# Softmax-band convolution and soft mixture of experts: softmax taps skewed by matmuls and GpSimd in place of a DRAM round trip

## The chip, the cores and the metric

The kernel runs on one core of one Trainium2 chip. The metric is device time in microseconds, the median of several executions. Everything is float32. A core has TensorE (PE; its weight loads are shown as PEld), VectorE (DVE), ScalarE (ACT), GpSimd (POOL) and SyncE (SP), which here only issues DMAs.

## The reference

Two layers follow each other. The first weights seven consecutive rows of `x` by a softmax over seven taps, separately for each token and head; the second is a soft mixture of experts.

```
# x: (8, 3584, 192); weight_gen: (8, 3584, 8 heads, 7 taps); a head has 24 channels
w   = softmax(weight_gen, axis=-1)                 # exp(w - max) / (sum + 1e-9)
out[b, s, head] = sum_k w[b, s, head, k] * x_padded[b, s + k, head]   # 6 zero rows ahead
x      = out.reshape(28672, 192)
logits = x @ phi                                   # 32 slots
d      = softmax over all tokens;  slot_in = d.T @ x
slot_out = relu(slot_in @ w1[e]) @ w2[e]           # 8 experts, 4 slots each
y      = softmax over slots(logits) @ slot_out
```

## The kernel before

**Tiling.** A batch has 35 groups of 4 x 26 = 104 tokens. A block is 26 tokens, which read 32 rows of `x`. Seven groups are a supergroup (40 in all), two groups are a pair (140 in all), eight pairs are a unit (17 units and a last one of four pairs). The convolution of a block and of four heads is one matmul: the weights are a band matrix of 128 x 26 (4 heads x 32 rows of `x`, by 26 tokens), the moving operand is the block's part of `x`, laid out block-diagonally by head in `xbd` (128 x 96). `conv(p)` issues 16 of them for pair p, which use the four column groups of the array side by side and write one of three PSUM buffers `cv`.

**A pair's path.** `conv(p)`, then `conv_out(p)` (ACT copies `cv` to `tm`), then `xpose(p)` (three TensorE transposes to `pt`) and `xpose_out(p)` (ACT copies to `cm`). Transposes run one pair behind the convolution. Per unit follow `logits` (16 matmuls to `ls`), `top` and `save` (DVE), `newmax` (a matmul to `pmx`), `newmax_out` (DVE), `dexp` (ACT), `dturn` (DVE), `dispatch` (16 matmuls to `ac`) and `rescale` (DVE). `soft` makes the softmax over slots per half batch, in steps on DVE (max), POOL (subtract), ACT (exp), DVE (sum, reciprocal) and POOL (multiply).

**The taps.** Taps arrive laid out by token. A band needs them skewed: row i of `x` holds tap i - j for token j. For the first two supergroups the kernel builds bands directly (`taps_*`, `band_mult`, DVE block transposes `band_turn`). For the others it works in chunks of two supergroups: `chunk_top` (DVE max), `chunk_sub` (POOL), `chunk_exp` (ACT), `chunk_sum` (POOL), `chunk_inv` (DVE), `chunk_norm` (POOL); then `send` writes the chunk to a DRAM buffer `via` with eight DMAs, each with the row offset that makes the skew, and `fetch` reads it back as `rows`, and `band_make` (DVE) multiplies `rows` by a mask that lies in the PSUM tile `pmx`:

```
SY.dma_start(via[ch % 2][q : q + 128].rearrange("(m k) s l -> m k s l", k=KS)
             [:, 0:KT, q], exps[ch % NEXP][q::KS, 0:KT])
```

**Order.** The engines' queues are written out by hand. A list `todo` of steps with planned times, made from `CONV`, `XPOSE`, `LOGITS`, `DISPATCH`, is sorted, and the steps are issued in that order; each engine runs its own in order, and semaphores hold it where an input is not there. The planned times set the order alone. SP issues all DMAs in the order of the list, so a DMA that waits holds up those behind it. `loadx(s + 2)` overwrites a buffer of `x` that supergroup s has finished with.

**The end.** After the last unit come the experts' small matmuls, and an output phase in which `rows` matmuls, copies on ACT and DVE and DMAs to the result alternate.

Of the kernel before, what the change touches and what calls it, by code (L numbers as in the profile page):

```python
# [8 lines left out]
F32 = mybir.dt.float32  # L9
# [7 lines left out]
KS = 8  # L17
FAR = -1e30
CG = 14
# [8 lines left out]
L = 2 * NBC  # L28
NCH = B * NG // CG
# [15 lines left out]
def conv_soft_moe(ctx, tc, xh, w0, wh, phi, w1a, w1b, w2, out):  # L45
# [15 lines left out]
    XB = 4 * NBC * GW  # L61
# [13 lines left out]
    def soft(pool, h, step):  # L75
        g0, n = HALVES[h]
        lt = LT[:, g0 : g0 + n, :]
        if step == 0:
            rms[h] = pool.tile([128, 18, 1], F32, tag="rm", name=f"rm{h}")[:, 0:n]
            V.tensor_reduce(out=rms[h], in_=lt, axis=AX.X, op=ALU.max)  # L80
        elif step == 1:
            G.tensor_tensor(out=lt, in0=lt, in1=rms.pop(h).to_broadcast([128, n, NS]),  # L82
                            op=ALU.subtract)
        elif step == 2:
            A.activation(lt, lt, AF.Exp)
        elif step == 3:
            sm = sms[h] = pool.tile([128, 18, 1], F32, tag="sm", name=f"sm{h}")[:, 0:n]
            sp = sm if pool is not pa else smP[h % 2][:, 0:n]
            V.tensor_reduce(out=sp, in_=lt, axis=AX.X, op=ALU.add)
            V.tensor_scalar_add(sm, sp, EPS)  # L90
            V.reciprocal(sm, sm)  # L91
# [13 lines left out]
    NXB, NTM, NCV, NRAW, NEXP, NBAND = 2, 2, 3, 2, 2, 3  # L105
    xbd = [big[:, i * XB : (i + 1) * XB].rearrange("p (h c) -> p h c", h=4) for i in range(NXB)]

    HB = NBC // 2
    WB = HB * 32
    early = w1a_sb.rearrange("p e f -> p (e f)")  # L110
    at = [0]

    def part(b, k):
        at[0] += b * k
        return early[:, at[0] - b * k : at[0]].rearrange("p (b k) -> p b k", k=k)

    wgs = [part(NBC, KS) for _ in range(2)]
    ens = [part(NBC, KS + 1) for _ in range(2)]
    wts = [part(HB, 32) for _ in range(2)]
    Ws = {(s, hf): part(HB, 32) for s in range(2) for hf in range(2)}  # L120

    raws = [fix.tile([128, L, KT], F32, name=f"raw{i}") for i in range(NRAW)]
    exps = [fix.tile([128, KS, L], F32, name=f"exp{i}") for i in range(NEXP)]
    rows8 = [fix.tile([128, KS, L], F32, name=f"rows{i}") for i in range(2)]
    bands = [fix.tile([128, HB, T, 2], F32, name=f"band{i}") for i in range(NBAND)]
    dram = actx.enter_context(tc.tile_pool(name="dram", bufs=1, space=bass.MemoryType.DRAM))
    via = [dram.tile([128 + KS, KS, L], F32, name=f"via{i}") for i in range(2)]

# [4 lines left out]

    pmx = ps_l.tile([128, 512], F32, name="pmx")
    pm, maskP = pmx[:, 0:5], pmx[:, 64:128].rearrange("p (i o) -> p i o", o=2)
    qnegP, q0P = pmx[:, 128:132], pmx[:, 132:133]
    smP = [pmx[:, 160 + 32 * i : 192 + 32 * i].rearrange("p (g o) -> p g o", o=1) for i in range(2)]
# [6 lines left out]
    G.memset(rows8[0], 0.0)  # L146
# [7 lines left out]
    for t in ens:  # L154
        V.memset(t[:, :, KS:], EPS)
    for t in exps:
        V.memset(t[:, KT], EPS)
    V.memset(xbd[0][:, 0, :], 0.0)
    V.memset(dd[:, 4:], 0.0)
    for h in (1, 2):  # L160
        G.memset(xbd[0][:, h, :], 0.0)
    A.copy(xbd[0][:, 3, :], zero.to_broadcast([128, NBC * GW]))
    A.copy(xbd[1][:, 0, :], zero.to_broadcast([128, NBC * GW]))
# [7 lines left out]
    maskT = keep.tile([128, 1, 32], F32, name="maskT")  # L171
    ident = keep.tile([128, 128], F32, name="ident")
    make_identity(nc, ident)

# [6 lines left out]
    mq = keep.tile([128, 5], F32, name="mq")  # L181

    for t in tms:
        V.memset(t[:, :, 0:1], 1.0)
        V.memset(t[:, :, 2 * D + 1 : 2 * D + 2], 1.0)
    V.memset(qneg, 0.0)
    V.memset(q0, 0.0)
    V.memset(q0[0:32], 1.0)
    for q in range(4):
        V.memset(qneg[32 * q : 32 * q + 32, q : q + 1], -1.0)  # L190

    def loadx(s):
        xb = xbd[s % NXB]
        for h in range(4):
            SY.dma_start(xb[32 * h : 32 * h + 32, h, :], xh[s, h])  # L195

    def loadw0(s):
        SY.dma_start(wgs[s], w0[s])

    def loadw(ch):  # L200
        SY.dma_start(raws[ch % NRAW], wh[ch - 1])

    tops, sums = {}, {}

    def chunk_top(ch):

        tops[ch] = pa.tile([128, L, 1], F32, tag="top", name=f"top{ch}")
        V.tensor_reduce(out=tops[ch][:, :, 0], in_=raws[ch % NRAW], axis=AX.X, op=ALU.max)  # L208

    def chunk_sub(ch, eng=G):  # L210
        raw = raws[ch % NRAW]
        eng.tensor_tensor(out=raw, in0=raw, in1=tops.pop(ch).to_broadcast([128, L, KT]),  # L212
                          op=ALU.subtract)

    def chunk_exp(ch):
        A.activation(exps[ch % NEXP][:, 0:KT], raws[ch % NRAW].rearrange("p b k -> p k b"), AF.Exp)  # L216

    def chunk_sum(ch, eng=G):
        e = exps[ch % NEXP]
        t = sums[ch] = pa.tile([128, 4, L], F32, tag="tree", name=f"sum{ch}", bufs=1)  # L220
        eng.tensor_tensor(out=t, in0=e[:, 0:4], in1=e[:, 4:KS], op=ALU.add)  # L221
        eng.tensor_tensor(out=t[:, 0:2], in0=t[:, 0:2], in1=t[:, 2:4], op=ALU.add)
        eng.tensor_tensor(out=t[:, 0], in0=t[:, 0], in1=t[:, 1], op=ALU.add)  # L223

    def chunk_inv(ch):
        t = sums[ch]
        V.reciprocal(t[:, 0], t[:, 0])  # L227

    def chunk_norm(ch, eng=G):
        w = exps[ch % NEXP][:, 0:KT]  # L230
        eng.tensor_tensor(out=w, in0=w, in1=sums.pop(ch)[:, 0:1].to_broadcast([128, KT, L]),  # L231
                          op=ALU.mult)

    def send(ch, lo=0, hi=KS):

        for q in range(lo, hi):
            SY.dma_start(via[ch % 2][q : q + 128].rearrange("(m k) s l -> m k s l", k=KS)  # L237
                         [:, 0:KT, q], exps[ch % NEXP][q::KS, 0:KT])

    def fetch(ch):  # L240
        SY.dma_start(rows8[ch % 2], via[ch % 2][0:128])

    def band_make(s):

        r = rows8[s // 2 % 2][:, :, s % 2 * NBC : (s % 2 + 1) * NBC]
        r = r.rearrange("p q (b o) -> p b q o", o=2)
        for j in range(0, T, KS):
            k = min(KS, T - j)
            V.tensor_tensor(out=bands[s % NBAND][:, :, j : j + k], in0=r[:, :, 0:k],  # L249
                            in1=maskP[:, j : j + k].rearrange("p (o q) t -> p o q t", o=1)  # L250
                            .to_broadcast([128, HB, k, 2]), op=ALU.mult)

    def taps_top(s, lo=0, n=NBC):
        mx = pa.tile([128, NBC, 1], F32, tag="wmx", name=f"wmx{s}_{lo}")[:, 0:n]
        V.tensor_reduce(out=mx[:, :, 0], in_=wgs[s][:, lo : lo + n], axis=AX.X, op=ALU.max)
        return mx

    def taps_exp(mx, s, lo=0, n=NBC, eng=V):
        en = ens[s][:, lo : lo + n, 0:KS]
        i = eng.tensor_tensor(out=en, in0=wgs[s][:, lo : lo + n],  # L260
                              in1=mx.to_broadcast([128, n, KS]), op=ALU.subtract)
        A.activation(en, en, AF.Exp)
        return i

    def taps_sum(s, lo=0, n=NBC):
        sm = pa.tile([128, NBC, 1], F32, tag="wsm", name=f"wsm{s}_{lo}")[:, 0:n]
        V.tensor_reduce(out=sm[:, :, 0], in_=ens[s][:, lo : lo + n], axis=AX.X, op=ALU.add)
        V.reciprocal(sm, sm)
        return sm

    def taps_norm(sm, s, lo=0, n=NBC, eng=G):
        en = ens[s][:, lo : lo + n, 0:KS]
        eng.tensor_tensor(out=en, in0=en, in1=sm.to_broadcast([128, n, KS]), op=ALU.mult)

    def band_mult(wt, s, at, lo, n, eng):
        wn = ens[s][:, at + lo : at + lo + n, 0:KS]
        eng.tensor_tensor(out=wt[:, lo : lo + n].rearrange("p b (a q) -> p b a q", q=KS),
                          in0=wn.rearrange("p b (o q) -> p b o q", o=1)
                          .to_broadcast([128, n, 32 // KS, KS]),
                          in1=mask.rearrange("p o (a q) -> p o a q", q=KS)  # L280
                          .to_broadcast([128, n, 32 // KS, KS]),
                          op=ALU.mult)

    def band_tiles(s, hf):
        return wts[(2 * s + hf) % 2], Ws[s, hf]

    turns = []
# [153 lines left out]
    for t in via:  # L441
        SY.dma_start(t[0:128], rows8[0])
# [444 lines left out]
```

## Time and profile before

| | |
|---|---|
| median of 3 executions | 410.22 us (410.08 to 415.51) |
| the profiled execution | 414.09 us, span 412.0 us |
| PE, DVE, ACT, POOL busy | 79%, 57%, 48%, 37% of the span |
| mean granted TensorE clock | 0.865 of full speed |
| bytes moved by DMA | 88.88 MB, mean 216 GB/s; 23792 of 43186 packets under 512 B |

The profile was taken of one execution, which lasted 414.09 us; its own span from the first to the last instruction is 412.0 us, and what is said of stages refers to it. Busy shares are averages over stages with different limits: a start until about 40 us, the convolution until about 328 us, then the experts and the output, where DMA moves about 400 GB/s.

### The profile page before, as it was taken

The numbers are of one execution on the slowest core, as the hardware profiler recorded it, in microseconds if no ns is written. First come the engines' busy times: TensorE is split into PE (matmuls) and PEld (weight loads), VectorE is DVE, ScalarE is ACT, GpSimd is POOL, SyncE is SP. The second block draws the span as 40 slices with busy tenths as digits, with TensorE's granted clock in tenths as the row PEclk, the third lists the DMA queues.
The fourth block names the chain that finished last, engine by engine and source line by source line (L and its number), as shares of the span: only waits on it lengthen the run. The fifth ranks groups of instructions, "written<-read, shape, count | busy, mean of one in ns | idle before, by whom it ended". The sixth has DMA issues, their size and how long they took to land.

```text
span 412.0 us, 15274 instructions
## 1 busy us (share of the span) xinstructions
PE 324.9 (79%) x6624; PEld 223.1 (54%) x6624; DVE 236.5 (57%) x500; ACT 199.1 (48%) x390; POOL 153.1 (37%) x147
## 2 busy tenths in 40 slices
PE   7664984949785986683989689789989998989940
PEld 7443663737563754463767467567767765323310
DVE  8954625464754682635567675567665354976540
ACT  7462453626444653443576565675566410634420
POOL 7732452527454563261545465543121142000000
PEclk9685898888988898977799999999999999995555
DMA  7547569698786798756488747766664690899996
GB/s 233 159 111 188 149 167 222 163 217 224 210 219 193 195 254 221 196 166 171 126 232 223 195 133 224 222 165 172 170 174 134 252 370 2 317 399 399 401 400 259
DMA packets 43186, 88.88 MB, mean 216 GB/s; under 512 B 23792, under 2 KB 24176, under 8 KB 43120
## 3 DMA queue, kind: packets, MB, share of 16 engines
q1 hardware_dynamic: 43120, 87.91, 71.0%
q8 instruction: 52, 0.85, 0.9%
q14 instruction: 14, 0.11, 0.1%
HBM read 56.98 MB, written 30.91 MB: 213 GB/s over the span
## 4 chain that ended last, share of the span: by engine, by line
PE 33%; DMA 27%; DVE 12%; SPq 11%; ACT 7%; issue 4%; POOL 3%; ACTq 0%; DVEq 0%; POOLq 0%
PE cv L312 10%; DMA via<-exp 8%; DMA out<-big 7%; PE pt L331 6%; DMA big<-xh 6%; PE ls L360 5%; SPq L195 5%; SPq L237 4%; PE ac L425 4%; DMA raw<-wh 4%; ACT exp L216 4%; DVE band L249 3%; PE po L771 2%; DMA w1b_sb<-w1b 2%; DMA rows<-via 2%
## 5 line engine op out<-in xcount | busy, mean ns | idle before, releaser
L312 PE MATMUL cv<-big,band 128*26 128x96 f32 x4256 | 125.9, 262 | 24.4 <-DMA big<-xh 10.8
L312 PEld LDWEIGHTS cv<-big,band 128*26 128x26 f32 x4256 | 97.7, 112 | 47.6 <-issue 24.9
L319 ACT COPY tm<-cv 128x384 f32<-128x384 f32 x140 | 67.2, 480 | 93.7 <-PE cv L312 93.1
L331 PE MATMUL pt<-ident,tm 122*128 122x122 f32 x420 | 80.3, 304 | 25.6 <-ACT tm L319 25.5
L249 DVE TENSOR_TENSOR band<-rows,pmx 128x448 f32<-128x448 f32 (+1 forms) x152 | 70.1, 523 | 31.7 <-DMA rows<-via 27.7
L331 PEld LDWEIGHTS pt<-ident,tm 122*128 122x128 f32 x420 | 47.7, 154 | 47.1 <-ACT tm L319 28.2
L336 ACT COPY cm<-pt 128x312 f32<-128x312 f32 x139 | 58.3, 420 | 3.3 <-PE pt L331 3.1
L216 ACT ACTIVATE exp<-raw 128x784 f32<-128x784 f32 x19 | 31.4, 1654 | 36.6 <-DMA via<-exp 31.8
L771 PE MATMUL po<-cT,so 32*128 32x442 f32 (+3 forms) x256 | 45.5, 785 | 2.0 <-ACT big L778 1.0
L231 POOL TENSOR_TENSOR exp<-exp,sum 128x784 f32<-128x784 f32 x18 | 33.5, 1860 | 29.4 <-DVE sum L227 14.1
L212 POOL TENSOR_TENSOR raw<-raw,top 128x784 f32<-128x784 f32 x18 | 28.2, 1565 | 34.3 <-DVE top L208 22.5
L778 ACT COPY big<-po 128x936 f32<-128x936 f32 (+1 forms) x24 | 21.8, 917 | 33.3 <-DMA out<-big 16.5
L221 POOL TENSOR_TENSOR sum<-exp 128x448 f32<-128x448 f32 x17 | 19.3, 1137 | 49.1 <-ACT exp L216 49.1
L778 DVE COPY big<-po 128x936 f32<-128x936 f32 (+1 forms) x24 | 26.1, 1095 | 16.6 <-DMA out<-big 12.5
L82 POOL TENSOR_TENSOR LT<-LT,rm 128x576 f32<-128x576 f32 (+1 forms) x16 | 18.1, 1131 | 41.9 <-DVE rm L80 41.9
L360 PE MATMUL ls<-cm,phi_sb 128*32 128x208 f32 (+1 forms) x576 | 30.3, 353 | 2.7 <-ACT cm L336 2.0
L771 PEld LDWEIGHTS po<-cT,so 32*128 32x128 f32 (+1 forms) x256 | 15.7, 202 | 30.6 <-ACT big L778 11.1
L425 PE MATMUL ac<-tm,dt 128*32 128x193 f32 x544 | 28.5, 350 | 1.1 <-issue 1.1
L227 DVE RECIPROCAL sum<-sum 128x112 f32<-128x112 f32 x19 | 16.0, 840 | 20.3 <-POOL sum L223 20.3
L93 POOL TENSOR_TENSOR LT<-LT,sm 128x576 f32<-128x576 f32 (+1 forms) x16 | 18.1, 1131 | 19.4 <-DVE sm L91 17.3
L367 DVE TENSOR_REDUCE mx<-ls 128x1 f32<-128x416 f32 (+1 forms) x18 | 10.3, 572 | 24.2 <-PE ls L360 24.2
L360 PEld LDWEIGHTS ls<-cm,phi_sb 128*32 128x32 f32 x576 | 17.3, 113 | 11.5 <-issue 2.5
(130 smaller groups left out, 293.0 us busy)
## 6 DMA issues: line engine op xcount, KB each, us to landing
big<-xh SPq DMA_DIRECT2D x160, 168.0 KB, 3.9
out<-big SPq DMA_DIRECT2D x24, 468.0 KB, 6.5
out<-big SPq DMA_DIRECT2D x24, 442.0 KB, 6.6
rows<-via SPq DMA_DIRECT2D x19, 448.0 KB, 5.2
raw<-wh SPq DMA_DIRECT2D x19, 392.0 KB, 5.8
via<-exp SPq DMA_DIRECT2D x152, 49.0 KB, 3.7
big<-w SPq DMA_DIRECT2D x7, 768.0 KB, 7.7
w1a_sb<-w1a SPq DMA_DIRECT2D x8, 512.0 KB, 4.3
```

The costliest lines, as they stand in the source:

```text
L212: eng.tensor_tensor(out=raw, in0=raw, in1=tops.pop(ch).to_broadcast([128, L, KT]), op=ALU.subtract)
L216: A.activation(exps[ch % NEXP][:, 0:KT], raws[ch % NRAW].rearrange("p b k -> p k b"), AF.Exp)
L231: eng.tensor_tensor(out=w, in0=w, in1=sums.pop(ch)[:, 0:1].to_broadcast([128, KT, L]), op=ALU.mult)
L249: V.tensor_tensor(out=bands[s % NBAND][:, :, j : j + k], in0=r[:, :, 0:k], in1=maskP[:, j : j + k].rearrange("p (o q) t -> p o q t", o=1) ...
L312: P.matmul(cv[32 * blk : 32 * blk + T, o : o + 96], Ws[s, bc // HB][:, bc % HB, 0:T] if s < 2 else bands[s % NBAND][:, bc // 2, :, bc % 2] ...
L319: A.copy(tms[u % NTM][:, pr, 1 : 2 * D + 1], cvs[p % NCV][:, 0 : 2 * D])
L331: P.transpose(pt[:, i, 0:TR], tm[0:TR, pr, 1 + 128 * i : 129 + 128 * i], ident[0:TR, 0:TR])
L336: copy(cms[u][:, pr].rearrange("p i b j -> p (i b) j"), pts.pop(p).rearrange("p i (b j) -> p (i b) j", j=32)[:, :, 0:T])
L360: P.matmul(lp[32 * blk : 32 * blk + 32, 0:n, par, 0:T], phi_sb[:, 2 * par + i, :], cm[:, 0:n, 1 if i else 2 * par, blk, :], start=(i == 0) ...
L425: P.matmul(ac[32 * q : 32 * q + 32], dt[:, g, :], tm[:, g // 2, o : o + D + 1], start=(g < 4), stop=(g + 4 >= 2 * n))
L771: P.matmul(po[dst : dst + hi - lo, q % 2, 0 : n * T], so[32 * q : 32 * q + 32, lo:hi], cT[32 * q : 32 * q + 32, g0 : g0 + n, 0:T], start=T ...
L778: (V.tensor_copy if done[1] % 2 else A.copy)(ot.rearrange("p (q c) -> p q c", q=2), po[:, :, 0 : n * T])
```

## The change

The DRAM buffer, `send`, `fetch`, the chunks and the separate start for two supergroups go. Every supergroup now follows one path:

- The host lays the taps out twice (`taps[:, 0]` by token as before, `taps[:, 1]` by row of `x`, so that the skew is in the input). One DMA `loadw(s)` brings both.
- `tap_top` (DVE) takes the maxima by token. `tap_rows` carries them to the rows with seven matmuls to the PSUM tile `pmx`, whose weights `sel` (128 x 128 each) are built at the start. `tap_sub` (DVE) subtracts, `tap_exp` (ACT) takes the exponential.
- `band_make` runs on POOL (parts of the first two supergroups on DVE) and multiplies the undivided exponentials by a 0/1 mask, now in SBUF, in two halves of two instructions each.
- `x` gets a 25th column of ones per head. The matmuls have 100 columns in place of 96, and the added column gives the sum of the undivided taps. `conv_sum` (ACT) copies the 16 sums of a pair and adds the epsilon; `conv_out` is now a DVE reciprocal of 16 numbers and a DVE multiplication of 384, from PSUM to `tm`.
- Transposes run three pairs behind the convolution (`LAG`). `loadx` is split in two parts, each issued when the groups that it overwrites are done. The epsilon of `soft` moves from DVE to ACT.

```diff
+    def tap_top(s):
+        tops[s] = pa.tile([128, NBC, 1], F32, tag="top", name=f"top{s}")
+        V.tensor_reduce(out=tops[s][:, :, 0], op=ALU.max, axis=AX.X,
+                        in_=taps[s % NTAP][:, 0].rearrange("p (l k) -> p l k", k=KT))
+    def tap_rows(s):
+        for q in range(KT):
+            P.matmul(topP[:, q], sel[:, q], tops[s][:, :, 0], start=True, stop=True)
+    def tap_sub(s):
+        r = taps[s % NTAP][:, 1].rearrange("p (b q o) -> p q b o", q=KT, o=2)
+        V.tensor_tensor(out=r, in0=r, in1=topP.rearrange("p q (b o) -> p q b o", o=2),
+                        op=ALU.subtract)
+    def tap_exp(s):
+        A.activation(taps[s % NTAP][:, 1], taps[s % NTAP][:, 1], AF.Exp)
...
-            V.tensor_tensor(out=bands[s % NBAND][:, :, j : j + k], in0=r[:, :, 0:k],
-                            in1=maskP[:, j : j + k].rearrange("p (o q) t -> p o q t", o=1)
-                            .to_broadcast([128, HB, k, 2]), op=ALU.mult)
+    def band_make(s, lo=0, hi=HB, eng=G):
+        r = taps[s % NTAP][:, 1].rearrange("p (b o q) -> p b o q", o=1, q=2 * KT)[:, lo:hi]
+        w = bands[s % NBAND][:, lo:hi].rearrange("p b j o -> p b (j o)")
+        m = mask2.rearrange("p j o -> p (j o)")
+        for j, a, k in ((0, 3, 2 * KT), (3 * KT, 1, 2 * (T - 3 * KT))):
+            z = slice(2 * j, 2 * j + a * k)
+            eng.tensor_tensor(out=w[:, :, z].rearrange("p b (a k) -> p b a k", k=k),
+                              in0=r[:, :, :, 0:k].to_broadcast([128, hi - lo, a, k]),
+                              in1=m[:, z].rearrange("p (b a k) -> p b a k", b=1, k=k)
+                              .to_broadcast([128, hi - lo, a, k]), op=ALU.mult)
...
-        A.copy(tms[u % NTM][:, pr, 1 : 2 * D + 1], cvs[p % NCV][:, 0 : 2 * D])
+        A.activation(wss[p], cvs[p % NCV][:, 0 : 16 * GX].rearrange("p (h w) -> p h w", w=GX)[:, :, GW:],
+                     AF.Identity, bias=eps[:, 0:1])
+        V.reciprocal(ws, ws)
+        V.tensor_tensor(out=tms[u % NTM][:, pr, 1 : 2 * D + 1].rearrange("p (h w) -> p h w", w=GW),
+                        in0=cv[:, :, 0:GW], in1=ws.to_broadcast([128, 16, GW]), op=ALU.mult)
...
-    CONV, XPOSE, LOGITS, DISPATCH = 0.82, 0.53, 1.7, 1.5
+    CONV, XPOSE, LOGITS, DISPATCH, ROWS = 0.8, 0.46, 1.5, 0.75, 0.5
+    LAG = 3
+    rowed = {begins[s] - 7: s for s in range(3, NSG)}
...
+        if p in rowed:
+            s = rowed[p]
+            at(t - 1.2, tap_top, s)
+            at(t, tap_rows, s)
+            t += ROWS
+            at(t + 0.1, tap_sub, s)
+            at(t + 0.7, tap_exp, s)
+            at(t + 1.4, band_make, s, 0, 14)
+            at(t + 3.4, band_make, s, 14, HB)
```

**TensorE, in a unit of the convolution.** `cv` rows are a pair's convolution, `pt` the transposes, `ls` the logits, `ac` the dispatch. Before:

```order
L331 MATMUL pt_1542<-ident,tm_97 128x122 x3
L425 MATMUL ac_1548<-tm_98,dt_1481 32x193 x16
L312 MATMUL cv_101<-big,band_92 26x96 x16
L331 MATMUL pt_1589<-ident,tm_97 128x122 x3
L312 MATMUL cv_102<-big,band_92 26x96 x16
L331 MATMUL pt_1612<-ident,tm_98 128x122 x3
L360 MATMUL ls<-cm_1338,phi_sb 32x8x26 x16
```

And now; `pmx<-top,sel` are the seven carrying matmuls (L182), and `pmx<-mq,sel` is `newmax`:

```order
L223 MATMUL cv_95<-big,band_90 26x100 x16
L253 MATMUL pt_1264<-ident,tm_92 128x122 x3
L182 MATMUL pmx<-top_1259,sel 128x56 x7
L304 MATMUL pmx<-mq,sel_139 128x5
L223 MATMUL cv_96<-big,band_90 26x100 x16
L253 MATMUL pt_1303<-ident,tm_92 128x122 x3
L223 MATMUL cv_94<-big,band_90 26x100 x16
L253 MATMUL pt_1340<-ident,tm_92 128x122 x3
L223 MATMUL cv_95<-big,band_90 26x100 x8
L223 MATMUL cv_95<-big,band_88 26x100 x8
L253 MATMUL pt_1378<-ident,tm_92 128x122 x3
L182 MATMUL pmx<-top_1370,sel 128x56 x7
```

Seven matmuls with weights of full width now stand between the pairs, once every three or four pairs; nothing else that TensorE does has gone.

**VectorE, at the same place** (`rm` and `dt` belong to `soft` and `dturn`, `nm` and `mq` to `newmax_out`). Before, where `band` is `band_make`:

```order
L249 TENSOR_TENSOR band_91<-rows_89,pmx 128x28x16 x3
L249 TENSOR_TENSOR band_91<-rows_89,pmx 128x28x4
L387 TENSOR_REDUCE nm_879<-pmx 128x1
L389 TENSOR_TENSOR mq<-nm_879,pmx 128x1
L80 TENSOR_REDUCE rm_882<-LT 128x18
L405 STREAM_TRANSPOSE dt_932<-dd 128x512
L227 RECIPROCAL sum_884<-sum_884 128x112
```

And now; `ws` and `tm` are the two instructions of an eviction, L186 is `tap_sub`, L176 `tap_top`:

```order
L186 TENSOR_TENSOR taps_86<-taps_86,pmx 128x7x28x2
L309 TENSOR_REDUCE nm_1299<-pmx 128x1
L311 TENSOR_TENSOR mq<-nm_1299,pmx 128x1
L239 RECIPROCAL ws_1313<-ws_1313 128x16
L240 TENSOR_TENSOR tm_92<-cv_96,ws_1313 128x384
L77 TENSOR_REDUCE rm_1336<-LT 128x17
L322 MEMSET dd 64x32
L324 MEMSET dd 32x4
L327 STREAM_TRANSPOSE dt_1348<-dd 128x512
L239 RECIPROCAL ws_1344<-ws_1344 128x16
L240 TENSOR_TENSOR tm_92<-cv_94,ws_1344 128x384
L176 TENSOR_REDUCE top_1370<-taps_87 128x56
```

Every pair's eviction now stands in VectorE's queue, and `tap_top`, on whose result the next L182 depends, stands behind them.

**SP's queue.** Before, for about three supergroups:

```order
L195 DMA big<-xh 32x1344 x4
L201 DMA raw_84<-wh 128x784
L237 DMA via_96<-exp_87 16x7x112 x4
L237 DMA via_95<-exp_86 16x7x112 x4
L629 DMA w1a_sb<-w1a 128x1024
L241 DMA rows_89<-via_96 128x896
```

And now:

```order
L169 DMA taps_87<-wh 128x784
L166 DMA big<-xh 32x600 x4
L517 DMA w1a_sb<-w1a 128x1024
L166 DMA big<-xh 32x800 x4
L169 DMA taps_84<-wh 128x784
```

The writes to `via` and the reads back are gone; the tap loads come once per supergroup in place of once per two.

419 lines of the change are left out of this document (142 added, 277 removed).

## The prediction

> **What bounds the kernel now.** I read the view by windows first, in four stages: the start, two parts of the convolution, and the end.
>
> ```profile
> core 0: us, PE busy (x) PEld busy (x) DVE busy (x) ACT busy (x) POOL busy (x), PEclk, DMA share, GB/s
> 0.00:40.00 40.00, 23.79 (x347) 19.20 (x347) 28.37 (x70) 20.42 (x32) 20.01 (x26) 0.76 0.63 177
> 40.00:200.00 160.00, 120.87 (x2702) 88.97 (x2702) 83.82 (x182) 77.49 (x160) 73.57 (x67) 0.85 0.75 198
> 200.00:328.00 128.00, 115.51 (x2983) 86.37 (x2980) 78.84 (x182) 75.85 (x167) 51.70 (x46) 0.99 0.65 181
> 328.00:412.00 84.00, 64.73 (x599) 28.51 (x598) 45.44 (x66) 25.34 (x33) 7.85 (x9) 0.74 0.82 320
> ```
>
> The 84 us of the last stage are not touched but for one microsecond below. How many pairs leave in each of the others, the same view shows for the eviction alone (L319):
>
> ```profile
> 0.00:40.00 40.00, 3.49 (x8) 0.76 0.63 177
> 40.00:200.00 160.00, 30.61 (x64) 0.85 0.75 198
> 200.00:328.00 128.00, 33.12 (x69) 0.99 0.65 181
> ```
>
> (One eviction straddles 40 us, so the pairs are 8, 63 and 69.) So a pair takes 160/63 = 2.54 us up to 200 us, and 128/69 = 1.86 us after it. What TensorE alone would take is read in the timeline of a late stretch at full clock:
>
> ```profile
> 317.34 0.87 PE L312 MATMUL cv<-big,band 128*26 128x96 f32 x32
> 318.60 0.86 PE L312 MATMUL cv<-big,band 128*26 128x96 f32 x32
> 319.86 1.51 PE L425 MATMUL ac<-tm,dt 128*32 128x193 f32 x32
> 321.19 0.84 PE L312 MATMUL cv<-big,band 128*26 128x96 f32 x32
> 323.69 1.61 PE L360 MATMUL ls<-cm,phi_sb 128*32 128x208 f32 x32
> 325.12 0.84 PE L312 MATMUL cv<-big,band 128*26 128x96 f32 x32
> 325.89 0.53 PE L331 MATMUL pt<-ident,tm 122*128 122x122 f32 x3
> 327.15 0.39 PE L382 MATMUL pmx<-mq,sel 128*128 128x5 f32 x2
> 327.39 0.96 PE L331 MATMUL pt<-ident,tm 122*128 122x122 f32 x6
> ```
>
> From start to start a pair is 1.26 us (convolution 0.80, transposes 0.46), dispatch 1.33, logits 1.43, newmax 0.24. A unit of eight pairs is 8 x 1.26 + 1.33 + 1.43 + 0.24 = 13.08 us, 1.64 us a pair. The last 132 pairs (16.5 units) would take 216 us and take 288: 72 us are waits and lost clock. The view of waits in 40 to 328 us names them:
>
> ```profile
> PEld pt L331 <- ACT tm L319: 26.0, 10, 6.4
> ACT exp L216 <- DMA via<-exp: 23.1, 6, 6.2
> DVE band L249 <- DMA rows<-via: 22.0, 4, 8.4
> PEld pmx L382 <- DVE band L249: 3.5, 6, 1.0
> ```
>
> TensorE waits for ACT's eviction, and ACT stands, in order, at an exponential whose buffer the DMAs to `via` have not yet read. One such place in the timeline:
>
> ```profile
> 129.13 1.60 ACT L216 ACTIVATE exp<-raw 128x784 f32<-128x784 f32 x1 [5.03 <-DMA via<-exp]
> 130.63 0.46 ACT L319 COPY tm<-cv 128x384 f32<-128x384 f32 x1
> ```
>
> So in the convolution the DRAM round trip bounds, through ACT's queue and through DVE's, and behind it TensorE.
>
> **What goes, and what comes.** With `via` go these waits, the DVE work on chunks (L249, L208, L227) and the chunk steps on POOL and ACT. The gain can at most be the 72 us. Against it stand three costs.
>
> *TensorE.* A pair now has 100 columns for 96: 0.80 x 4/96 = 0.03 us. Seven carrying matmuls per supergroup load 128 columns of weights each, in two passes; `fill` does the same:
>
> ```profile
> 333.44 0.74 PEld L637 LDWEIGHTS fill<-ident 128*128 128x128 f32 x6 [0.31 <-issue]
> L637 PEld LDWEIGHTS fill<-ident 128*128 128x128 f32 x12 | 1.5, 190 | 0.6 <-issue 0.6
> ```
>
> Six loads take 0.74 us with a last one of 0.19, so one starts every 0.11 us, and 14 take 1.54 us; the moving side has only 56 columns and hides in it. By L382 above (0.24 us for one such matmul of two passes) it would be 1.68. I take 1.56, bounds 1.5 and 1.8. A unit has 8/3.5 = 2.29 supergroups: 13.08 + 8 x 0.03 + 2.29 x 1.56 = 16.9 us, 2.11 us a pair. 16.5 units: 279 us in place of 216. So 63 of the 72 us come back as TensorE work.
>
> *VectorE.* Rows for its new work:
>
> ```profile
> L249 DVE TENSOR_TENSOR band<-rows,pmx 128x448 f32<-128x448 f32 x114 | 63.2, 609 | 31.7 <-DMA rows<-via 27.7 <-PE pmx L382 2.0 <-DMA big<-xh 1.9
> L249 DVE TENSOR_TENSOR band<-rows,pmx 128x112 f32<-128x112 f32 x38 | 10.0, 264 | 0.0
> L227 DVE RECIPROCAL sum<-sum 128x112 f32<-128x112 f32 x19 | 16.0, 840 | 20.3 <-POOL sum L223 20.3
> L91 DVE RECIPROCAL sm<-sm 128x18 f32<-128x18 f32 x8 | 2.1, 266 | 0.3
> L208 DVE TENSOR_REDUCE top<-raw 128x112 f32<-128x784 f32 x19 | 17.9, 943 | 0.0
> L405 DVE STREAM_TRANSPOSE dt<-dd 128x512 f32<-128x512 f32 x17 | 12.0, 707 | 5.3 <-ACT dd L393 5.0
> L80 DVE TENSOR_REDUCE rm<-LT 128x18 f32<-128x576 f32 x8 | 5.9, 742 | 0.0
> ```
>
> An eviction is a multiplication of 384 (between the two L249 forms: 0.54 us) and a reciprocal of 16 (between L91 and L227: 0.25), with the hand-over about 0.84. `tap_top` of 392 is 0.56 (L208 and L80), `tap_sub` 0.55. Per unit: 8 x 0.84 + 2.29 x 1.11 + 2.9 for the unit's own (`top`, `save`, `newmax_out`, `dturn`, `rescale`: two transposes of 0.71 and five shorter) + 1.6 for 0.91 half batches of `soft` = 13.8 us. That is 82% of TensorE's 16.9: not the bound by its sum, but in a strict order. I followed one unit through both queues, from the carry of one supergroup to the next, counted from the carry's start. TensorE: carry 1.56, newmax 0.24, three pairs 3 x 1.29: the next carry is wanted at 5.7 us. VectorE: `tap_sub` and `newmax_out` end at 2.85, ACT's `dexp` and sums at 3.75, eviction 4.65, `rm` 5.4, `dturn` 6.25, eviction 7.1, `tap_top` 7.7. The carry starts 2.0 us late. Without the half batch of `soft` in that stretch it is 0.2 to 0.3 us late per carry. That makes some 0.5 us in a good unit and 2.2 in one like this, which I put at 1.1 on average: 18 us. Bounds: 0.3 per unit (5 us), and the share that the late stage shows now, 1.86/1.64 = 13.5%, with less VectorE work (38 us).
>
> *POOL and ACT* have room. Bands cost, by
>
> ```profile
> L221 POOL TENSOR_TENSOR sum<-exp 128x448 f32<-128x448 f32 x17 | 19.3, 1137 | 49.1 <-ACT exp L216 49.1
> L82 POOL TENSOR_TENSOR LT<-LT,rm 128x576 f32<-128x576 f32 x8 | 9.3, 1158 | 23.2 <-DVE rm L80 23.2
> L411 ACT ACTIVATE al<-nm,nm 128x1 f32<-128x1 f32 x17 | 5.2, 307 | 0.0
> ```
>
> 2.0 to 2.5 ns an element, so 2.9 to 3.7 us for a band's 1456 elements, of the 7.4 us that a supergroup takes on TensorE; with `soft` 0.9 more. The band is begun two supergroups ahead. ACT exchanges a copy of 0.48 for `conv_sum` of about 0.32 (L411). On SP the two loads of `x` come half a supergroup earlier in use and have 1.5 supergroups, 11 us, to land; I count no wait there. If these covers fail, each late load costs TensorE what it is late.
>
> *The start.* Now the ninth pair waits for the round trip until 40 us. After: the warm-up matmuls end near 8.5 us,
>
> ```profile
> 7.63 0.83 PE L153 MATMUL warm<-dd 128*128 128x128 f32 x6
> ```
>
> then carry (1.6, twice that at the half clock of a waiting TensorE), `tap_sub`, `tap_exp` and a first band piece: first pair near 13 us in place of 10.6. Supergroups 1 and 2 follow by the same chain, 8 us each (carry 1.6 to 3, `tap_sub` and `tap_exp` 1.1, band 3.7): bands at 21.5 and 30 us, the eighth pair out at about 34 us, bounds 31 and 36. That gains 6.
>
> *The sum.* 34 + 279 + 18 = 331 us at the end of the convolution, for 328 now; then two more transposes (2 x 0.46) stand behind the last pair: +4 us. The profiled execution took 414.09 us, 3.9 more than the median, so its 418 stand for **414 us** on the scale of the 410.22 median.
>
> **Two rules weighed.** The clock was 0.85 in the stage with the long waits and 0.99 in the one without; my sum uses durations at full clock. The Trainium skill ("TensorE: Matmul & The Clock Gate", Part 1) says that the clock falls to half after an idle window of about 3.4 us and returns after one of work; by that the new waits of 2 us keep it full, and the sum stands. If 0.85 stayed for the first 63 pairs, as a row alone might suggest, it would add 63 x 2.11 x 0.18 = 24 us.
>
> `newmax` waited six times, 3.5 us in all, for DVE reading another part of the tile `pmx`. The Trainium skill ("PSUM — Partial Sum Buffer", Terms) says that two engines may not use one bank and quadrant at once; `tap_rows` now writes that bank, so each may wait for a DVE read. At 0.6 us each that would be 23 us for 38 carries, where I count 18 for all waits: 419 us.
>
> **The rivals.** *Faster.* The carries are hidden or the waits stay small: 31 + 279 + 8 = 318, so 401 us; if even the loads hide behind the transposes (the planner's own `ROWS` is 0.5 us) DVE's 13.8 us per unit set the pace, and it is below 385. For it: evictions have two pairs of slack. Against: in the L382 row the next matmul starts a full 0.24 us after it, so nothing of that one was hidden.
>
> *Slower: VectorE's order decides.* `tap_top` stands behind evictions, and an eviction behind a wait for ACT; then every carry is late by what one unit above shows once. With 1.95 us at half of 38 carries, 37 us: 34 + 279 + 37 = 350, so 433 us. It decides from 22 us of waits on (4.4 more than the 18 that I count make 418.4). For it: VectorE is at 82%, where it was at 62% of the late stage and TensorE still lost 13.5%. Against: the late stage also lost time to loads of `x`, now issued earlier.
>
> **How the numbers follow.** Forecast, within 2% (402 to 418.4, about what a measurement of this kernel can tell from no change): 0.36, 414 us, by itself 403 to 424. Faster by over 2%: 0.29, of which 0.04 for hidden loads. Slower by over 2%: 0.35. The range holds start (-3, +2), carry (0, +10) and waits (-13, +20) together, cut where no more than 2 in 10 are left out: 396 to 434.
>
> **What would show it.** Right: no DMA among TensorE's long waits; granted clock near 1.0 from 50 us on; L182 at about 1.56 us per seven; the eighth eviction near 34 us; a pair every 2.2 to 2.3 us throughout, faster than before up to 200 us and slower than before after it; carries that wait for `tap_top`. Wrong: seven carries in under 1 us, or gaps before L182 above 1 us in most supergroups, or POOL's bands ending TensorE's waits.

## The result, and the profile after

The changed kernel takes **429.01 us** (median of 4, 427.80 to 431.88), the kernel before beside it 410.37: a ratio of 1.043, 95% interval 1.034 to 1.053, so slower by more than 2%. The forecast of 414 us was 15 us low; the time lies inside the range of 396 to 434, in the part that was there for the slower rival. The profiled execution took 427.80 us (span 426.1). Medians are taken over all executions, ratios over those in the faster of the two states that executions come in, so the two can differ a little.

The view by windows of the changed kernel, cut at 40, 200 and the convolution's end, and below it the eviction alone (L240, now on DVE):

```profile
core 0: us, PE busy (x) PEld busy (x) DVE busy (x) ACT busy (x) POOL busy (x), PEclk, DMA share, GB/s
0.00:40.00 40.00, 30.96 (x422) 27.58 (x426) 20.53 (x61) 14.72 (x31) 14.80 (x25) 0.79 0.49 137
40.00:200.00 160.00, 150.66 (x3240) 121.39 (x3232) 105.21 (x262) 63.62 (x186) 86.05 (x94) 0.97 0.63 179
200.00:338.10 138.10, 130.06 (x2911) 104.56 (x2903) 94.99 (x240) 58.63 (x172) 71.99 (x78) 1.00 0.50 139
338.10:426.10 88.00, 66.43 (x639) 30.00 (x628) 46.89 (x69) 27.00 (x38) 7.84 (x9) 0.76 0.80 312
```
```profile
40.00:200.00 160.00, 38.19 (x69) 0.97 0.63 179
200.00:338.10 138.10, 35.01 (x63) 1.00 0.50 139
```

A pair takes 160/69 = 2.32 us up to 200 us (before 2.54) and 138.1/63 = 2.19 after it (before 1.86): faster in the first part, slower in the second, as foretold. TensorE is now busy for 94% of both stretches; before it was 76% of the first and 90% of the second. Its waits in 37 to 338 us, in the view of waits (us in total, times, longest):

```profile
PE pmx L182 <- DVE top L176: 13.9, 16, 1.8
PE pmx L182 <- DVE mq L311: 1.9, 4, 0.5
PE ac L347 <- DVE dt L327: 1.2, 3, 0.6
```

No DMA is among them; what is left is nearly all `tap_rows` (L182) waiting for `tap_top` (L176). The changed kernel's timeline at full clock gives the price of a carry, and one of the long waits shows what stands in front of it on DVE:

```profile
42.52 1.77 PE L182 MATMUL pmx<-top,sel 128*128 128x56 f32 x14
44.22 0.89 PE L223 MATMUL cv<-big,band 128*26 128x100 f32 x32
...
48.41 0.89 PE L223 MATMUL cv<-big,band 128*26 128x100 f32 x32
49.69 0.89 PE L223 MATMUL cv<-big,band 128*26 128x100 f32 x32
```
```profile
88.23 0.71 DVE L327 STREAM_TRANSPOSE dt<-dd 128x512 f32<-128x512 f32 x1
88.86 0.21 DVE L239 RECIPROCAL ws<-ws 128x16 f32<-128x16 f32 x1
89.18 0.56 DVE L240 TENSOR_TENSOR tm<-cv,ws 128x384 f32<-128x384 f32 x1
89.65 0.55 DVE L176 TENSOR_REDUCE top<-taps 128x56 f32<-128x392 f32 x1
90.26 3.06 PEld L182 LDWEIGHTS pmx<-top,sel 128*128 128x128 f32 x14 [2.03 <-DVE top L176]
```

From the start of its first load, here at the same time as the first matmul's, to the start of the next work a carry is 44.22 - 42.52 = 1.70 us and a pair 1.28. `tap_top` comes behind a transpose and an eviction, the carry waits 2.03 us on its loads, and then its 14 loads take 3.06 us instead of 1.6: the granted clock, 1.00 until 90.3 us, is 0.50 from there to 97.1 us.

### The profile page after: what moved, and what is told of

Same layout as the page of the kernel before. It is cut to its first block, busy times and chain, and to the rows that moved or that the text cites. A ratio compares the mean times of both kernels' runs of the same rounds, so it can differ in the third digit from the quotient of the medians.

```text
span 426.1 us, 16874 instructions
## 1 busy us (share of the span) xinstructions
PE 378.1 (89%) x7184; PEld 283.5 (67%) x7184; DVE 267.6 (63%) x631; ACT 164.0 (38%) x424; POOL 180.7 (42%) x206
## 4 chain that ended last, share of the span: by engine, by line
PE 59%; DVE 22%; DMA 6%; ACT 4%; issue 3%; SPq 2%; DVEq 0%; POOL 0%; ACTq 0%; POOLq 0%
PE pmx L182 17%; PE cv L223 15%; PE pt L253 7%; PE ls L282 7%; DVE tm L240 6%; PE ac L347 6%; DMA out<-big 6%; DVE top L176 3%; PE po L661 2%; DVE ws L239 2%; SPq L670 2%; DVE mx L289 2%; DVE LT L295 2%; ACT dd L315 2%; PE hp L609 1%
## 5 line engine op out<-in xcount | busy, mean ns | idle before, releaser
L199 POOL TENSOR_TENSOR band<-taps,mask 128x140 f32<-128x140 f32 (+2 forms) x156 | 137.8, 913 | 120.1 <-issue 91.7
L223 PE MATMUL cv<-big,band 128*26 128x100 f32 x4480 | 128.1, 255 | 3.5 <-POOL band L199 3.5
L182 PE MATMUL pmx<-top,sel 128*128 128x56 f32 x560 | 74.6, 288 | 20.7 <-DVE top L176 18.3
L182 PEld LDWEIGHTS pmx<-top,sel 128*128 128x128 f32 x560 | 69.8, 202 | 28.2 <-DVE top L176 24.9
L240 DVE TENSOR_TENSOR tm<-cv,ws 128x384 f32<-128x384 f32 x140 | 78.2, 559 | 15.0 <-PE pmx L182 0.5
L253 PE MATMUL pt<-ident,tm 122*128 122x122 f32 x420 | 74.9, 288 | 0.0
L239 DVE RECIPROCAL ws<-ws 128x16 f32<-128x16 f32 x140 | 33.6, 240 | 40.6 <-ACT ws L232 39.2
L232 ACT ACTIVATE ws<-cv,eps 128x16 f32<-128x16 f32 x140 | 37.5, 268 | 52.5 <-PE cv L223 51.6
L190 ACT ACTIVATE taps<-taps 128x392 f32<-128x392 f32 x40 | 21.2, 530 | 90.8 <-DVE taps L186 90.8
L186 DVE TENSOR_TENSOR taps<-taps,pmx 128x392 f32<-128x392 f32 x40 | 22.5, 563 | 35.9 <-PE pmx L182 33.0
L282 PEld LDWEIGHTS ls<-cm,phi_sb 128*32 128x32 f32 x576 | 16.5, 109 | 8.2 <-ACT ws L232 1.3
```

What stands on the lines that cost most here:

```text
L182: P.matmul(topP[:, q], sel[:, q], tops[s][:, :, 0], start=True, stop=True)
L199: eng.tensor_tensor(out=w[:, :, z].rearrange("p b (a k) -> p b a k", k=k), in0=r[:, :, :, 0:k].to_broadcast([128, hi - lo, a, k]), in1=m[: ...
L223: P.matmul(cv[32 * blk : 32 * blk + T, o : o + 4 * GX], bands[s % NBAND][:, bc // 2, :, bc % 2], xb[:, :, bc * GX : (bc + 1) * GX], start= ...
L232: A.activation(wss[p], cvs[p % NCV][:, 0 : 16 * GX].rearrange("p (h w) -> p h w", w=GX)[:, :, GW:], AF.Identity, bias=eps[:, 0:1])
L239: V.reciprocal(ws, ws)
L240: V.tensor_tensor(out=tms[u % NTM][:, pr, 1 : 2 * D + 1].rearrange("p (h w) -> p h w", w=GW), in0=cv[:, :, 0:GW], in1=ws.to_broadcast([128 ...
```

## The experiments

All times are medians; "eighth eviction" is its start and "pairs" is the time from the eighth eviction to the last, in the profiled execution, and the ratio is to the kernel before on the same chip. In every kernel with the new layout, 87.9 to 89.3 us of the span follow the last eviction's start; in the kernel before 84.7, and 85.3 without its writes to the buffer. The runs come from several chips, on which the kernel before has medians of 407.46 to 410.37 us; a difference of 3 us between kernels from different chips says little by itself.

| kernel | us | ratio (95%) | eighth eviction | pairs |
|---|---|---|---|---|
| before | 410.37 | | 39.9 | 287.4 |
| changed | 429.01 | 1.043 (1.034 to 1.053) | 37.0 | 301.1 |
| tap_top early | 405.82 | 0.994 (0.990 to 0.998) | 35.3 | 280.7 |
| one matmul of seven | 397.04 | 0.972 (0.963 to 0.981) | 36.0 | 270.4 |
| one weight load | 397.74 | 0.976 (0.967 to 0.985) | 37.9 | 273.0 |
| no maxima | 351.40 | 0.861 (0.854 to 0.868) | 26.5 | 236.6 |
| tap_top and taps early | 400.80 | 0.989 (0.983 to 0.995) | 36.0 | 275.1 |
| the same, one matmul | 374.48 | 0.928 (0.917 to 0.938) | 35.4 | 249.9 |
| one weight load, taps early | 382.82 | 0.949 (0.938 to 0.961) | 36.5 | 259.0 |
| before, nothing sent | 373.61 | 0.923 (0.906 to 0.940) | 34.0 | 252.5 |
| new start | 380.15 | 0.937 (0.927 to 0.946) | 34.4 | 255.6 |
| new start, spreading on DVE | 377.21 | 0.923 (0.918 to 0.928) | 31.3 | 254.7 |

### The place of tap_top

```diff
-            at(t - 1.2, tap_top, s)
+            at(t - 4.0, tap_top, s)
```

> Only the place of tap_top in VectorE's queue changes: its due time is 4.0 us ahead of the carry in place of 1.2. Theory (VectorE's strict order makes the carries late): the 16 waits of L182 for L176 that the trace shows (13.9 us on PE, 19.8 us on its loads between 37 and 338 us) go, and with them the stretch of half clock behind the longest; 429 becomes 408 to 414. Rival (VectorE is simply too full, at 82% of a unit): the waits only change their name, to evictions or to L311, and the time stays at 424 to 430.

405.82 us, more than the theory gave: one due time in VectorE's order is worth 23 us. The eighth eviction comes 1.7 us earlier and the pairs lose 20 us: the 15.8 us that L182 waited on PE, and the half clock behind two of these waits (5 us, worked out below), less a few waits that are new. What TensorE still waits for in 37 to 318 us adds up to 5 us and no longer names L176:

```profile
PE pt L253 <- ACT cm L258: 2.4, 2, 2.0
PE ac L347 <- DVE dt L327: 2.1, 3, 0.8
PE pmx L304 <- DVE mq L291: 0.6, 2, 0.4
```

The rival, a VectorE that is too full, falls: its work is the same.

### Fewer matmuls in the carry

```diff
-        for q in range(KT):
+        for q in range(KT if s < 3 else 1):
             P.matmul(topP[:, q], sel[:, q], tops[s][:, :, 0], start=True, stop=True)
```

> From supergroup 3 on only one of the seven carrying matmuls is issued (six slices of topP keep old maxima, so the taps are shifted by wrong values); VectorE, ScalarE and GpSimd do all that they did. Theory (the seven carries' weight loads stand on the path at 1.70 us per supergroup): 6/7 of 1.70 us for 37 supergroups, 54 us, leaves TensorE, and it reaches 429 - 54 = 375 if nothing else binds, up to 390 with more waits for tap_top. Rival (VectorE's 13.8 us per unit and its order set the pace): less than half is gained, 403 or more.

397.04 us: 32 of 54 us, between the two. `tap_top` is at its old place, and the shorter carries wait for it longer, in 20 places on PE instead of 16:

```profile
PE pmx L182 <- DVE top L176: 20.7, 20, 2.1
```

So the matmuls are on the path, and so is VectorE's order.

The next kernel carries all maxima with one weight load. Its multiplication on GpSimd is a step of its own, `tap_spread`, due 4.0 us ahead of the matmul, with `tap_top` due 5.0 us ahead (`<...>` stands for an access pattern):

```diff
-        for q in range(KT):
-            P.matmul(topP[:, q], sel[:, q], tops[s][:, :, 0], start=True, stop=True)
+        G.tensor_tensor(out=spread[s], in0=<tops[s] over 7 slices>, in1=<own over 56 columns>, op=ALU.mult)
+        P.matmul(pmx[:, 0:TAPS], sel, <spread[s], 392 columns>, start=True, stop=True)
```

> All maxima are carried, with one weight load: GpSimd first spreads the 56 maxima over seven slices (times the column own), and one matmul of 392 columns with the unmasked band as weights does the sum of rows; tap_top goes to 5.0 us and the spreading to 4.0 us ahead of it. Theory (weight loads are the price of the carry): two passes of 392 columns at the 0.86 ns a column of dispatch's matmuls are 0.7 us in place of 1.70, 37 us over 37 supergroups, and the waits for tap_top go as in the run with the earlier tap_top: 429 - 37 - 17 = 375, up to 390. Rival (GpSimd becomes late: 3.54 us of band, 0.9 of soft and about 0.9 of spreading are 5.3 of a supergroup's 6.6 us): waits for the band appear in front of L223 and the time is 400 or more.

397.74 us: neither reason. The carry did shrink, but bands were not late; `tap_top`, now due 5.0 us ahead, ran into its own DMA, and stopped VectorE. The view of waits and the timeline of this kernel:

```profile
DVE top L176 <- DMA taps<-wh: 26.1, 16, 3.7
```
```profile
69.23 0.56 DVE L176 TENSOR_REDUCE top<-taps 128x56 f32<-128x392 f32 x1 [2.93 <-DMA taps<-wh]
...
70.84 0.70 DVE L336 STREAM_TRANSPOSE dt<-dd 128x512 f32<-128x512 f32 x1
...
71.59 2.10 PEld L356 LDWEIGHTS ac<-tm,dt 128*32 128x32 f32 x32 [3.53 <-DVE dt L336]
```

`dturn` stands behind `tap_top`, and dispatch (L356 here) behind `dturn`: 3.53 us for a load of taps. An instruction that is moved forward takes its own inputs' deadline with it.

### No maxima

```diff
-            at(t - 1.2, tap_top, s)
-            at(t, tap_rows, s)
-            t += ROWS
-            at(t + 0.1, tap_sub, s)
```

(The same three steps go at the start, and `ROWS` is 0.0 in the planned times.)

> The taps go to the exponential without their maxima: tap_top, the seven matmuls and tap_sub are left out, bands, column sums and division stay. It prices everything that the maxima cost in this layout. Theory (carry and its waits are nearly the whole loss): TensorE has 13.4 us a unit, 16.5 units are 221 us, start about 30 and end 88: 339 us without waits, 345 to 360 with some. Rival (the division at eviction on VectorE, not the carry, is what costs): 0.84 us a pair stays, evictions are late and the time is 385 or more.

351.40 us, as the theory had it. The maxima cost 78 us of the changed kernel; of the 75.1 us between the two profiled executions, 10.6 lie ahead of the eighth eviction and 64.5 in the pairs. The division at eviction stays in this kernel and is no obstacle. (It prices the carry, its waits and VectorE's two instructions together; without maxima the exponential has no guard against large taps.)

### The load of the taps, with seven matmuls, one, and one weight load

Three kernels share this edit; the first has the seven matmuls, the second one of them, the third the spreading:

```diff
             if part == 0 and s + 4 < NSG:
-                at(t + 0.02, loadw, s + 4)
+                at(start[max(begins[s] - 1, first)], loadw, s + 4)
...
-            at(t - 1.2, tap_top, s)
+            at(t - 3.2, tap_top, s)
```

> Seven matmuls as in the changed kernel; tap_top due 3.2 us ahead of them and the taps loaded earlier, as in the run beside it. It separates the load of the taps from the weight loads. If the load was late for the run with the earlier tap_top too (it waited 9.6 us for it in 7 places on VectorE, of which TensorE saw some 4): 399 to 404 us. If VectorE had slack for it: 404 to 408, no change against 405.82.

400.80 us: the load was late there too. This kernel is the clean measure of the carry, since TensorE waits for almost nothing in 37 to 300 us:

```profile
PE ac L347 <- DVE dt L327: 0.6, 2, 0.3
PE cv L223 <- issue: 0.4, 1, 0.4
PE pmx L182 <- issue: 0.3, 1, 0.3
```

Its pairs take 275.1 us, which is nearly TensorE's own work. The changed kernel's 301.1 are 26.0 more: that is the price of the order, its waits and the half clock behind them.

> As the run beside it with early tap_top and taps, and one of the seven matmuls from supergroup 3 on (stale maxima in the other six slices, so other shifts). Theory (the seven carries stand on TensorE's path in full once VectorE's order is right): 1.70 to 0.36 us per carry, 36 times, 48 us: 352 to 362. Rival (VectorE's work is the next bound close by): 375 or more, so that under 30 us of the 48 are gained.

374.48 us: 26 of the 48 us come back, which is the rival's condition (under 30), though the time is a little below its 375. Pairs take 249.9 us, and the next waits are spread thin, the largest of them:

```profile
PE ac L347 <- DVE dt L327: 7.8, 13, 0.9
PE cv L223 <- POOL band L199: 3.7, 1, 3.7
PE ls L282 <- ACT cm L258: 2.9, 3, 1.0
```

> As the run with one weight load (397.74 us, whose tap_top waited 26.1 us for the load of the taps), but the load of the taps of supergroup s + 4 is issued one pair before supergroup s, ahead of two loads of x instead of behind the first, and tap_top is due 3.2 and the spreading 2.4 us ahead of the matmul. Theory (VectorE stood at tap_top for a late DMA, and dispatch behind it): those waits go, and the carry's 0.86 in place of 1.70 us counts in full, 36 times: the 405.82 us of the run with the earlier tap_top become 370 to 380. Rival (VectorE, 13.8 us per unit, cannot follow a TensorE of 15 us per unit): 388 or more, with waits of TensorE for dturn, top or evictions.

382.82 us: between both, 18 us less than with seven matmuls, of 30 that the loads would give; TensorE's waits in 37 to 300 us, 1.3 us with seven matmuls, are 10.1 here, the largest for `x` (4.5). VectorE no longer waits for taps. A carry in the timeline of this kernel, again from its first load to the next work, is 36.85 - 35.99 = 0.86 us, for all maxima:

```profile
35.99 0.30 PEld L190 LDWEIGHTS pmx<-spread,sel 128*128 128x128 f32 x2
36.09 0.83 PE L190 MATMUL pmx<-spread,sel 128*128 128x392 f32 x2
...
36.85 0.67 PEld L232 LDWEIGHTS cv<-big,band 128*26 128x26 f32 x32 [0.56 <-DVE ws L248]
```

### What the DRAM buffer had cost

```diff
     def send(ch, lo=0, hi=KS):
-        for q in range(lo, hi):
-            SY.dma_start(<via, shifted by q rows>, exps[ch % NEXP][q::KS, 0:KT])
+        return
```

> The kernel before without the DMAs that write the exponentials to the DRAM buffer: the buffer keeps its zeros, so from supergroup 2 on the bands are zeros; the loads from it, and all steps of the engines, stay. Theory (the round trip alone bounds the convolution before): the waits of ScalarE and VectorE for it go, up to 72 us minus some 10 that remain to other waits: 348 to 365. Rival (ScalarE's and GpSimd's chunk steps or VectorE's bands hold TensorE back as well): 385 or more.

373.61 us: 31 us gained by the ratio, 36 by the medians, so at most half of the 72. The clock comes back (0.98 in 40 to 200 us, before 0.85), and the pairs take 252.5 us; but other waits step in, for ACT's eviction and for `x` (the view by windows, and the view of waits):

```profile
40.00:200.00 160.00, 136.77 (x3489) 101.67 (x3479) 107.68 (x236) 96.75 (x201) 91.51 (x82) 0.98 0.72 208
```
```profile
PE pt L329 <- ACT tm L317: 9.2, 11, 1.5
PE cv L310 <- DMA big<-xh: 8.9, 10, 1.5
```

So writing to the buffer cost 31 to 36 us, the seven matmuls that took its place are 61 us of TensorE (36 carries of 1.70 in the stretch of the pairs). The loads back from the buffer stay in this kernel and were not priced apart.

### Both kernels once more

> The kernel before once more, with a profile. If its times scatter because the waits for the DRAM buffer do, another profiled execution differs from 414.09 us by several us, and the difference lies between 40 and 328 us, in the waits for the DMAs to and from the buffer. If the profiler adds a fixed 3.9 us to this kernel, it is 414 again.

> The changed kernel once more, with a profile. Its waits come from the order alone: the same 2.0 us waits for tap_top at the same carries, and a time within 2 us of 427.8. Whether the clock falls to half behind the first of these waits again (0.51 for 7 us), behind another or behind none is open; each fall would cost 3.5 us.

The kernel before took 406.21 us this time, 7.9 less than its first profiled execution, and 8.1 of it are in the pairs (279.3 for 287.4). The waits for the buffer are fewer, the longest of them longer:

```profile
ACT exp L216 <- DMA via<-exp: 27.4, 5, 8.9
PEld pt L331 <- ACT tm L319: 25.1, 12, 6.1
DVE band L249 <- DMA rows<-via: 17.0, 3, 8.7
```

Over all runs of this study it took 401.4 to 415.5 us. The changed kernel took 428.80, with the same 2.0 us waits at the same three carries. In all, TensorE's waits in the pairs are 6.6 us shorter than in the first profiled execution (45.3 for 51.9), but the waits of ScalarE and VectorE for the buffer, in the first and third line, add up to nearly the same (44.4 for 45.1). So the kernel before takes 8 us more or less from one profiled execution to the next, without a fixed amount added by the profiler; that the buffer's DMAs cause it isn't shown, since kernels without them scatter too: the one with `tap_top` early took 404.09 to 411.36 us.

### The start

```diff
     loadw(1)
+    loadw(2)
     SY.dma_start(phi_sb, phi)
+    loadw(3)
...
     band_make(0, 20, HB, V)
+    tap_rows(1)
+    tap_top(2)
+    tap_spread(2, V)
+    tap_sub(1)
+    tap_exp(1)
...
     conv(0)
...
     conv_out(0)
+    tap_rows(2)
```

(The same calls and the loads are removed at their old places; `tap_sub(2)` and `tap_exp(2)` move ahead of `conv(1)`.)

> As the run with one weight load and early taps (382.82 us), with another order of the start: taps 2 and 3 are loaded ahead of the second supergroup of x, the maxima of supergroup 1 are carried ahead of the first pair, those of supergroup 2 right behind it, and supergroup 2's taps are reduced by their maxima ahead of the second eviction. Theory (the start is a chain of carry, exponential and band per supergroup, and TensorE can follow it): bands 1 and 2 are ready some 5 us earlier and the eighth eviction comes at 28 to 31 us in place of 36.5: 375 to 378 us. Rival (the second and third supergroup of x land no earlier, so the ninth pair waits for them): 381 to 384.

380.15 us, 2.7 gained where 5 to 8 were hoped for; neither fits well, and the eighth eviction comes at 34.4 us, not at 28 to 31. Band 2 is ready 2.9 us earlier than in the kernel that this one starts from (24.9 for 27.8 us), band 1 is not (20.3 for 19.4), and `x` was there; the next carry waited instead, since on GpSimd the spreading of supergroup 3 stood behind band 2:

```profile
25.73 1.68 PE L190 MATMUL pmx<-spread,sel 128*128 128x392 f32 x2 [4.47 <-POOL spread L183]
```

```diff
-            at(t - 2.4, tap_spread, s)
+            at(t - 2.4, tap_spread, s, V if s == 3 else G)
```

> As the run with the new start (380.15 us), with one instruction on another engine: the spreading of supergroup 3's maxima goes from GpSimd, where it stood behind 3.48 us of band 2, to VectorE. Theory (that wait of 4.47 us and the half clock behind it are what is left of the start): the third carry starts near 23 us in place of 25.7, and the time is 375 to 378 us. Rival (bands 2 and 3 on GpSimd or the loads of x for supergroup 2 set the start anyway): 379 to 381.

377.21 us, as the theory had it; the same carry starts at 22.49 us and the eighth eviction comes at 31.3:

```profile
22.49 1.68 PE L190 MATMUL pmx<-spread,sel 128*128 128x392 f32 x2 [3.11 <-DVE spread L183]
```

This version keeps the maxima and beats the kernel before (ratio 0.923) and the changed one.

## Why the prediction was right or wrong, point by point

The time lies inside the range, but nearer to the slower rival's 433 us than to the 414 that were given, and "slower by over 2%" had a chance of 0.35 beside the forecast's 0.36. The mechanism was foreseen. The number was not: the start, the waits with the clock and the end came out longer than computed, the scale had taken 5 us too many off, TensorE's own work was a little shorter, and the range held all this because the slower rival had made it wide. (Its lower end, 396, lies 2 us below what its own terms give: 414 - 3 - 13 = 398.)

**What bounds before: right in kind, half in size.** The waits named the round trip, and without the writes ScalarE's go and VectorE's fall from 22.0 to 11.0 us. But "the gain can at most be the 72 us" was read as what the buffer costs; without the writes 31 to 36 us were gained.

**TensorE's sum: right, in part by luck.** 279 us for 132 pairs; the kernel almost without waits has 275.1. A single carry was sized too small, 1.70 us for 1.56: the loads do start every 0.11 us, but the next work starts only 0.21 us behind the last matmul's start. There are 36 carries in that stretch where 16.5 units had been taken to hold 37.8, so that two errors nearly cancelled (61 and 59 us).

**The pieces on VectorE and GpSimd: right.** The groups of the changed kernel, one form a line, have 0.56 + 0.24 us for an eviction (0.54 + 0.25 foretold), 0.55 for `tap_top` (0.56), and 2 x (1.35 + 0.48) = 3.66 for a band (2.9 to 3.7):

```profile
L240 DVE TENSOR_TENSOR tm<-cv,ws 128x384 f32<-128x384 f32 x140 | 78.2, 559 | 15.0 <-PE pmx L182 0.5
L239 DVE RECIPROCAL ws<-ws 128x16 f32<-128x16 f32 x140 | 33.6, 240 | 40.6 <-ACT ws L232 39.2
L176 DVE TENSOR_REDUCE top<-taps 128x56 f32<-128x392 f32 x40 | 22.0, 550 | 0.0
L199 POOL TENSOR_TENSOR band<-taps,mask 128x588 f32<-128x588 f32 x77 | 103.8, 1348 | 113.5 <-issue 91.7 <-ACT taps L190 16.2 <-DVE sm L88 3.0
L199 POOL TENSOR_TENSOR band<-taps,mask 128x140 f32<-128x140 f32 x77 | 37.2, 483 | 0.0
```

**VectorE's order: the right mechanism and nearly the right size.** Forecast: 18 us of waits. Measured: 17.0 us on PE, and 26.0 us between this kernel and one with the order mended. Some 5 of these are the clock, below; the other 4 are not traced one by one, but the loads of the carries wait longer than their matmuls (19.8 us in 24 places for `tap_top`, 13.9 in 16 on PE). The rival that wanted 37 us of waits, 1.95 us at every second carry, did not happen: a wait of 2 us occurs three times, most are under 1.1 us. Yet what that rival named, VectorE's order, decides whether the change costs time: with `tap_top` early the ratio is 0.994. The price that the order may have without turning the result was smaller than the 22 us put on it, since the start, the end and the scale had used up the rest.

**The clock: wrong by 5 us.** The forecast took full clock for granted "by the new waits of 2 us". It is 0.97 in 40 to 200 us, and the windows of 7 us behind the three longest waits show why:

```profile
90.20:97.20 7.00, 6.94 (x78) 5.80 (x78) 2.51 (x7) 0.77 (x3) 2.28 (x4) 0.51 0.63 201
166.50:173.50 7.00, 6.94 (x115) 5.63 (x116) 3.37 (x9) 1.54 (x5) 2.86 (x4) 0.76 0.16 41
295.50:302.50 7.00, 6.94 (x151) 5.60 (x151) 4.36 (x11) 2.27 (x7) 3.69 (x4) 1.00 0.42 111
```

Half clock for 7 us, for about half of that, and not at all: 3.4 + 1.7 = 5 us of work lost, not 24 and not none. The Trainium skill ("TensorE: Matmul & The Clock Gate", Part 1) has the clock fall after an idle window of about 3.4 us, and the prediction read it as sparing waits of 2 us; here the clock fell behind two of three waits of 2.0 us, in the second execution of this kernel behind the same two. The same section calls the window free-running. The granted clock in the trace fits that: it is 0.50 from 90.28 to 97.11 us and from 168.79 to 172.20 us, 6.83 = 2 x 3.413 us and 3.41 us, and the two falls lie 78.51 = 23 x 3.413 us apart. How little work in such a window is enough stays open: in the 3.41 us ahead of the two falls TensorE was busy for 1.60 and 2.23 us, and for 2.06 us in the window that holds most of the third wait (291.67 to 295.08), behind which the clock stayed.

**The shared bank.** The carries' waits for L311, which reads the same tile, are 1.9 us in 4 places, not 0.6 at each of 38: the 23 us that the prediction weighed for one bank and quadrant did not come.

**The start: 3 us short.** The bands came as computed: band 1 ends at 18.99 + 1.85 = 20.8 us (21.5 foretold), band 2 at 26.67 + 3.50 = 30.2 (30 foretold). What failed is the step from there to "eighth pair at about 34": TensorE's pairs stand, in order, behind the carry of the next supergroup, and that one behind `tap_top`, which stands behind a band and an eviction on DVE:

```profile
18.99 1.85 DVE L199 TENSOR_TENSOR band<-taps,mask 128x588 f32<-128x588 f32 x2
...
21.58 0.55 DVE L176 TENSOR_REDUCE top<-taps 128x56 f32<-128x392 f32 x1
22.19 3.06 PEld L182 LDWEIGHTS pmx<-top,sel 128*128 128x128 f32 x14 [3.93 <-DVE top L176]
25.35 2.51 PEld L223 LDWEIGHTS cv<-big,band 128*26 128x26 f32 x64
26.67 3.50 POOL L199 TENSOR_TENSOR band<-taps,mask 128x588 f32<-128x588 f32 x4 [5.99 <-ACT taps L190]
```

The third and fourth pair wait until 25.35 us for a carry that they don't need. The eighth eviction came at 37.0 us.

**The end: 2 us short.** The changed order puts 88.0 us behind the last eviction, 84.7 before; +1 was foretold.

**The scale: 5 us.** The sum was 418 us on the scale of the profiled execution, and 3.9 us were taken off because the kernel before's profiled execution lay that far above its median. That was no property of the profile but scatter: another profiled execution lay below the median. The changed kernel's profiled execution was 1.2 us below its median, and 3.9 + 1.2 = 5.1 of the 15 us come from this step alone. The others: start 3, pairs 4 (297 for 301), end 2; rounding the rest. The 4 us of the pairs hide two larger errors, 8 too few for waits and clock (18 for 26) and 4 too many for TensorE's own work (279 for 275), so the largest error of the sum is the one in waits and clock.

**Covers.** ACT, POOL and SP held up as said: in 37 to 338 us no band of POOL's and no load of `x` ends a wait of a TensorE matmul (weight loads waited 0.5 us in all for a band).

## What to carry to other kernels

When a stage's waits are swapped for work on the engine that bounds, price the waits by taking them out (31 to 36 us here) and not by adding them up (72), and count the new work in full: 61 us of weight loads were bought for 31 to 36. Before giving up such a change, look at the one instruction that the new work waits for: an order written by hand is worth as much as the mechanism (23 us here), and the instruction that is moved forward must have its own inputs moved too. Data that moves across partitions by matmul was cheaper here as one wide moving operand (0.86 us, and a GpSimd multiplication that lays it out) than as seven narrow ones with weights of their own (1.70 us).

## What the hardware showed

In these traces a VectorE multiplication with two SBUF inputs and a GpSimd one slow each other down. In the start of the changed kernel two DVE band pieces take 1.85 us (above) beside two of GpSimd; in the start of the kernel with the new start the same pieces of band 1 do not overlap:

```profile
18.39 2.29 POOL L199 TENSOR_TENSOR band<-taps,mask 128x588 f32<-128x588 f32 x2 [5.53 <-ACT taps L190]
```
```profile
15.67 1.77 POOL L208 TENSOR_TENSOR band<-taps,mask 128x588 f32<-128x588 f32 x2 [2.72 <-ACT taps L199]
...
19.30 0.99 DVE L208 TENSOR_TENSOR band<-taps,mask 128x588 f32<-128x588 f32 x2
```

1.85 for 0.99 and 2.29 for 1.77: side by side they take 2.45 us from first to last, one behind the other 2.76. The Trainium skill ("SBUF — State Buffer", SBUF: two separate sides) describes a pair of ports that one of the two engines holds for a whole instruction while the other waits. The trace agrees nearly: of the four pieces only the one that started first keeps its time (1.34 us on GpSimd in both kernels), VectorE's take 1.36 and 0.57 us in place of 0.77 and 0.30, GpSimd's second 1.00 in place of 0.47, and a band split over both engines gains 0.3 us and not half.
